# K and V caches loaded one head at a time, or two heads interleaved over the partitions: a decode block with sliding-window attention and a gated MLP

## The chip, the cores and the metric

The kernel runs on one core of one Trainium2 chip. The metric is the device time of one execution in microseconds (us). Each engine of the core has its own queue of instructions: PE multiplies matrices (PEld is its loading of the stationary operand), DVE is the vector engine, ACT the scalar engine, POOL the general engine, SP the sync engine, which here issues nearly all DMA transfers. One transfer is spread over 16 DMA engines. SBUF is the on-chip memory with 128 partitions, PSUM the memory that PE writes into.

## The reference

One token (a row x of 576 values) is normalised, goes through an attention block and through a gated MLP, and both results are added to x:

```
xn  = layernorm(x)                                   # 576
q   = xn @ wq                                        # 32 heads of 128
k,v = the last 4096 rows of each of 16 cached heads  # 128 columns, two q heads share one k, v head
p   = softmax(q . k / sqrt(128));  o = p @ v         # per head
A   = o (4096) @ wo                                  # 576
z   = gelu(xn @ w_in)                                # 4608, halves z1, z2
B   = (z1 * (w_sp * layernorm(z2) + b_sp)) @ w_out   # 2304 -> 576
out = x + A + B
```

All tensors are bfloat16. A cached head is a region of 65536 rows of 256 bytes, 16 MiB. Its last 4096 rows, 1 MiB, are read. K and V together are 33.5 MB of the 51 MB that the kernel reads; the rest is wq (4.7 MB), w_in (5.3 MB), wo (4.7 MB) and w_out (2.7 MB). A transfer's "row" below is the contiguous piece that one partition receives.

## The kernel before, in words

The order of the work is written out by hand. All large loads are issued by SP, in one queue and in a fixed order (lines 105 to 118): K of the first pair of heads, all of wq, then for each pair b = 1 to 8 the next K, the V of the pair before, and a piece of w_in (b = 1 to 3) or of wo (b = 4 to 6); after the last K come the last piece of wo, the last V, and w_out. Loads land in a pool of 18 units of one size (UNITS, line 34), taken in turn: a load waits until the unit's old content has been read. Besides, at most eight transfers are in flight at a time, which is how the kernel's tile library gives out its DMA semaphores.

`load_kv` (line 79) loads one head: partition p gets the 32 consecutive cache rows 32p to 32p+31, 8192 bytes. `load_rows` (line 92) loads two rows per partition of wq (8192 bytes) or of w_in (9216 bytes), or eight of w_out (9216 bytes), the last piece being smaller: one row of wq (4096 bytes) and of w_in (4608), two of w_out (2304).

Each pair of heads goes through these steps, in eight chunks n of eight 128x128 blocks:

- `T(n)` (line 199): eight transposes of K on PE into PSUM, then a copy to SBUF by DVE (five chunks of eight) or ACT (three). Three PSUM buffers serve all chunks.
- `S(n)` (line 210): eight matmuls with a transposed K block as the stationary operand and the two q columns of that head as the moving one. They fill the pair's score tile s, 128 partitions x (2 heads, 32 blocks, 2 queries).
- `sm_max`, `sm_tr`, `sm_exp`, `sm_rec` (lines 219 to 253): the maximum over the blocks (mx, DVE), over the partitions (a transpose on PE and a reduction), its broadcast by a small matmul (bc), then the difference d (DVE), the exponential p (ACT), the sums ss (DVE), and their total over the partitions by a matmul on PE (su), whose reciprocal is rm.
- `PV(b, i)` (line 255): 32 matmuls for head i of the pair, with a V block as the stationary operand and two columns of p as the moving one, accumulated in the tile o. `O(b)` scales it.

The main loop (lines 361 to 391) is a pipeline on PE: the transposes of pair b, with the scores of pair b two chunks behind, the total su of pair b-1 after the second chunk, then P V of pair b-1, whose second half hides the maximum of pair b, then in stages 1 to 3 `z_part(b)` (line 289: 18 matmuls for each row of w_in that has landed, four rows, four rows and one row), then the rest of pair b's softmax. Every second stage permutes the attention output (`O_perm`, tiles op and oP), and stages 4, 5, 6 and 8 multiply it with a piece of wo (`WO`). At the end 72 small matmuls (line 393) add the MLP's output from w_out's 18 rows, and the result is copied and stored. Before the loop, PE makes the eight chunks of the first pair and computes q row by row of wq (lines 336 to 341), 16 matmuls for each row.

Of the kernel before, what the change touches and what calls it, by code (L numbers as in the profile page):

```python
# [8 lines left out]
FP32 = mybir.dt.float32  # L9
BF16 = mybir.dt.bfloat16  # L10
ALU = mybir.AluOpType
ACT = mybir.ActivationFunctionType
AXX = mybir.AxisListType.X

P = 128
D = 576
HQ = 32
HKV = 16
DH = 128
SK = 65536  # L20
W = 4096
FH = 2304
NT = W // P
NB = HKV // 2
NCH = 8
NS = 9
# [4 lines left out]
OW = D // NCG  # L31
NWO = 4
FR = FH // P
UNITS = 18
KTB = 12


@with_exitstack
def kernel(
# [14 lines left out]
    nc = tc.nc  # L54
    ctx.enter_context(tc.manual_schedule())

    const = ctx.enter_context(tc.tile_pool(name="const", bufs=1))
    work = ctx.enter_context(tc.tile_pool(name="work", bufs=2))
    units = ctx.enter_context(tc.tile_pool(name="units", bufs=UNITS))
    ktp = ctx.enter_context(tc.tile_pool(name="ktp", bufs=KTB))  # L60
    PS = bass.MemoryType.PSUM
    ps_t = ctx.enter_context(tc.tile_pool(name="ps_t", bufs=3, space=PS))
    ps_s = ctx.enter_context(tc.tile_pool(name="ps_s", bufs=2, space=PS))
# [9 lines left out]
    kn, vn, wq_t, win_t, wo_t, wout_t = {}, {}, {}, {}, {}, {}  # L73
    wq_v = A_wq.rearrange("k (s c) -> (k s) c", s=2).rearrange("(p r) c -> p r c", r=NS)
    win_v = B_w_in.rearrange("k (s c) -> (k s) c", s=2).rearrange("(p r) c -> p r c", r=NS)
    wo_v = A_wo.rearrange("(j p r) n -> j p (r n)", p=P, r=8)
    wout_v = B_w_out.rearrange("(p r) n -> p r n", r=FR)

    def load_kv(store, cache, name, h):
        t = units.tile([P, NT, DH], BF16, name=f"{name}{h}", tag="u")  # L80
        nc.sync.dma_start(t[:], cache[0, h, SK - W:SK, :].rearrange("(p t) d -> p t d", p=P))
        store[h] = t

    def load_k(b):
        for i in range(2):
            load_kv(kn, A_k_cache, "k", 2 * b + i)

    def load_v(b):
        for i in range(2):
            load_kv(vn, A_v_cache, "v", 2 * b + i)  # L90

    def load_rows(store, view, name, width, rows, step):
        for a in range(rows.start, rows.stop, step):
            n = min(step, rows.stop - a)
            t = units.tile([P, step, width], BF16, name=f"{name}{a}", tag="u")
            nc.sync.dma_start(t[:, 0:n, :], view[:, a:a + n, :])
            for i in range(n):
                store[a + i] = t[:, i, :]

    def load_wo(j):  # L100
        t = units.tile([P, 8 * D], BF16, name=f"wo{j}", tag="u")
        nc.sync.dma_start(t[:], wo_v[j])
        wo_t[j] = t

    win_parts = {1: range(0, 4), 2: range(4, 8), 3: range(8, 9)}
    load_k(0)
    load_rows(wq_t, wq_v, "wq", 2048, range(0, NS), 2)
    for b in range(1, NB + 1):
        if b < NB:
            load_k(b)  # L110
        else:
            load_wo(NWO - 1)
        load_v(b - 1)
        if b in win_parts:
            load_rows(win_t, win_v, "win", FH, win_parts[b], 2)
        elif b < 7:
            load_wo(b - 4)
    load_rows(wout_t, wout_v, "wout", D, range(0, FR), 8)


    ident = const.tile([P, P], BF16, name="ident")
# [5 lines left out]
    ones_f = const.tile([P, P], FP32, name="ones_f")  # L127
    nc.vector.memset(ones_f[:], 1.0)
    ident_f = const.tile([P, P], FP32, name="ident_f")
# [2 lines left out]
    nc.vector.tensor_reduce(out=par[:], in_=ident_f[:].rearrange("p (m s) -> p s m", s=2), axis=AXX, op=ALU.add)  # L132
    hm = const.tile([P, 8], FP32, name="hm")
    nc.vector.tensor_reduce(out=hm[:], in_=ident_f[:].rearrange("p (n q) -> p n q", n=8), axis=AXX, op=ALU.add)
    selr = const.tile([P, 8, 8, 16], BF16, name="selr")
    out_ps = ps_c.tile([P, OW], FP32, name="out_ps")
    nc.vector.memset(out_ps[:], 0.0)
# [7 lines left out]
    for j in range(NS):  # L145
# [11 lines left out]
                                   op0=ALU.mult, op1=ALU.add, accum_out=stat[:, 1:2])  # L157
# [29 lines left out]
    def xe_of(r):  # L187
        return xe_r[:, 2 * r:2 * r + 2]
# [4 lines left out]
    kT, s_ps, p_sb, sm = {}, {}, {}, {}  # L193
    q_bf = const.tile([P, HQ], BF16, name="q_bf")
# [2 lines left out]
    ACT_COPIES = (1, 4, 6)  # L197

    def T(n):
        h, c = divmod(n, 4)  # L200
        kT[n] = ktp.tile([P, 8, P], BF16, name=f"kT{n}", tag="kT")
        tp = ps_t.tile([P, 8, P], BF16, name=f"tp{n}", tag="tp")
        for i in range(8):
            nc.tensor.transpose(tp[:, i, :], kn[h][:, 8 * c + i, :], ident[:])  # L204
        if n % 8 in ACT_COPIES:
            nc.scalar.copy(kT[n][:], tp[:])  # L206
        else:
            nc.vector.tensor_copy(kT[n][:], tp[:])  # L208

    def S(n):  # L210
        h, c = divmod(n, 4)
        b, i = divmod(h, 2)
        if n % NCH == 0:
            s_ps[b] = ps_s.tile([P, 2, NT, 2], FP32, name=f"s{b}", tag="s")
        for t in range(8):
            nc.tensor.matmul(s_ps[b][:, i, 8 * c + t, :], lhsT=kT[n][:, t, :], rhs=q_bf[:, 2 * h:2 * h + 2],  # L216
                             start=True, stop=True)

    def sm_max(b):
        mx = work.tile([P, 2, 2], FP32, name=f"mx{b}", tag="mx")  # L220
        nc.vector.tensor_reduce(out=mx[:], in_=s_ps[b][:].rearrange("p i t r -> p i r t"), axis=AXX, op=ALU.max)  # L221
        sm[b] = {"mx": mx}

    def sm_tr(b):
        tr = ps_m.tile([P, P], FP32, name=f"tr{b}", tag="m")
        nc.tensor.transpose(tr[0:4, :], sm[b]["mx"][:].rearrange("p i r -> p (i r)"), ident_f[:])  # L226
        m4 = work.tile([4, 1], FP32, name=f"m4{b}", tag="m4")
        nc.vector.tensor_reduce(out=m4[:], in_=tr[0:4, :], axis=AXX, op=ALU.max)  # L228
        dg = work.tile([4, 4], FP32, name=f"dg{b}", tag="dg")
        nc.vector.tensor_scalar_mul(dg[:], ident_f[0:4, 0:4], m4[:])  # L230
        sm[b]["dg"] = dg

    def sm_exp(b):
        bc = ps_m.tile([P, 4], FP32, name=f"bc{b}", tag="m")
        nc.tensor.matmul(bc[:], lhsT=ones_f[0:4, :], rhs=sm[b]["dg"][:], start=True, stop=True)  # L235
        mb = work.tile([P, 4], FP32, name=f"mb{b}", tag="mb")
        nc.vector.tensor_copy(mb[:], bc[:])
        d = work.tile([P, 2, NT, 2], FP32, name=f"d{b}", tag="d")
        m = mb[:].rearrange("p (i r) -> p i r", i=2).unsqueeze(2).to_broadcast([P, 2, NT, 2])
        nc.vector.tensor_tensor(out=d[:], in0=s_ps[b][:], in1=m, op=ALU.subtract)  # L240
        p = work.tile([P, 2, NT, 2], BF16, name=f"p{b}", tag="p")
        nc.scalar.activation(p[:], d[:], ACT.Exp, scale=SCALE)  # L242
        p_sb[b] = p
        ss = work.tile([P, 2, 2], FP32, name=f"ss{b}", tag="ss")
        nc.vector.tensor_reduce(out=ss[:], in_=p[:].rearrange("p i t r -> p i r t"), axis=AXX, op=ALU.add)  # L245
        sm[b]["ss"] = ss

    def sm_rec(b):
        su = ps_m.tile([P, 4], FP32, name=f"su{b}", tag="m")
        nc.tensor.matmul(su[:], lhsT=ones_f[:], rhs=sm[b]["ss"][:].rearrange("p i r -> p (i r)"), start=True, stop=True)  # L250
        rm = work.tile([P, 4], FP32, name=f"rm{b}", tag="rm")
        nc.vector.reciprocal(rm[:], su[:])
        sm[b]["rm"] = rm

    def PV(b, i):
        if i == 0:
            sm[b]["o"] = ps_o.tile([P, 4], FP32, name=f"o{b}", tag="o")
        for t in range(NT):
            nc.tensor.matmul(sm[b]["o"][:, 2 * i:2 * i + 2], lhsT=vn[2 * b + i][:, t, :], rhs=p_sb[b][:, i, t, :],  # L259
                             start=t == 0, stop=t == NT - 1)  # L260

    def O(b):
        with nc.allow_low_precision(reason="the attention's output is bfloat16 in the reference"):
# [23 lines left out]
    zacc = const.tile([P, FR, 2], FP32, name="zacc")  # L287

    def z_part(b):
        rows = win_parts[b]  # L290
        zp = ps_m.tile([P, FR, 2], FP32, name=f"zp{b}", tag="m")
        for r in rows:
            w_r = win_t[r].rearrange("p (m c) -> p c m", c=FR)
            for c in range(FR):
                nc.tensor.matmul(zp[:, c, :], lhsT=w_r[:, c, :], rhs=xe_of(r), start=(r == rows.start and c == 0),  # L295
                                 stop=r == rows.stop - 1, skip_group_check=True)
        if b == 1:
            nc.vector.tensor_copy(zacc[:], zp[:])
        else:
            nc.vector.tensor_tensor(out=zacc[:], in0=zp[:], in1=zacc[:], op=ALU.add)  # L300
# [60 lines left out]
    for b in range(1, NB + 1):  # L361
# [66 lines left out]
```

## Time and profile before

| what | value |
|---|---|
| median of 3 runs | 132.65 us (132.42 to 132.65) |
| the profiled execution | 132.56 us, its span 130.8 us |
| read from HBM | 50.96 MB, 390 GB/s over the span |
| PE busy, PEld busy | 103.5 us, 98.1 us |
| DVE, ACT busy | 51.8 us, 29.1 us |
| mean granted clock of PE | 0.73 of full speed |
| from issue to landing of a K or V transfer | 20.4 us |

The profile shows one execution. Its span begins with the first recorded instruction and ends with the last; 1.76 us of the execution's time lie outside it. The page cuts the span into 40 slices of 3.27 us. It gives each slice a digit for the busy share in tenths of every engine and of the DMA engines, the moved GB/s, and the granted clock of PE in tenths. The timeline lists instructions in the order of time (start, duration, engine, line, result <- operands, count); what stands in brackets is the engine's idle time before, and what ended it. A group's line gives the busy time, the mean of one in ns, and the idle time before. In the table of windows, the columns are the stretch, its length, busy time and count of PE, PEld, DVE, ACT and POOL, PE's granted clock, the DMA share and GB/s. A line of the waits reads: who waited, for whom, us in total, times, longest.

### The profile page before, as it was taken

What the parts mean: (1) busy time and instruction counts of PE and PEld (TensorE: products, weight loads), DVE (VectorE), ACT (ScalarE), POOL (GpSimd) and SP (SyncE); (2) the same over time, 40 slices, a digit from 0 to 9 for tenths busy, and PEclk for the clock granted to TensorE, in tenths of its full rate; (3) what the DMA queues carried; (4) which work ended last, traced back from release to release, by engine and by line L of the source; (5) the groups of instructions that cost most, each with busy time, mean ns of one, the idle gap of its engine ahead of it and who ended that gap; (6) DMA issues with size and microseconds to landing.
All of it is one profiled execution on the core that took longest, in us unless ns stands there. A gap on an engine that the chain in (4) does not pass through costs nothing.

```text
span 130.8 us, 4611 instructions
## 1 busy us (share of the span) xinstructions
PE 103.5 (79%) x2133; PEld 98.1 (75%) x2133; DVE 51.8 (40%) x157; ACT 29.1 (22%) x38; POOL 0.7 (1%) x6
## 2 busy tenths in 40 slices
PE   3587238699799998989977897899599869975760
PEld 3487227499698998989976896799499759964750
DVE  4495000345402543054537544654426434542100
ACT  3135000045000360005404140236025103500000
POOL 2000000000000000000000000000000000000000
PEclk9999955559955589657975568569959955995555
DMA  3999999999999999999999999999999999999820
GB/s 93 436 421 423 428 407 427 411 425 432 411 413 421 421 417 418 411 423 413 418 421 415 424 409 423 415 430 411 426 418 418 419 416 415 419 418 421 364 118 0
DMA packets 7088, 51.24 MB, mean 392 GB/s; under 512 B 797, under 2 KB 798, under 8 KB 1182
## 3 DMA queue, kind: packets, MB, share of 16 engines
q1 hardware_dynamic: 7064, 50.96, 94.2%
q8 instruction: 16, 0.26, 0.8%
q14 instruction: 2, 0.02, 0.0%
q10 hardware_dynamic: 6, 0.00, 0.0%
HBM read 50.96 MB, written 0.00 MB: 390 GB/s over the span
## 4 chain that ended last, share of the span: by engine, by line
DMA 63%; PE 31%; DVE 2%; issue 1%; SPq 0%
DMA k<-in_A_k_cache_dram 19%; DMA v<-in_A_v_cache_dram 17%; DMA wout<-in_B_w_out_dram 16%; PE tp L204 12%; DMA wq<-in_A_wq_dram 12%; PE zp L295 7%; PE s L216 4%; PE o L259 3%; PE bc L235 1%; PE out_ps L278 1%; PE su L250 1%; DVE m L228 1%; PE q_ps L339 0%; PE tr L226 0%; PE op L269 0%
## 5 line engine op out<-in xcount | busy, mean ns | idle before, releaser
L204 PE MATMUL tp<-ident,k 128*128 128x128 bf16 x512 | 50.1, 265 | 1.4 <-DMA k<-in_A_k_cache_dram 0.8
L204 PEld LDWEIGHTS <-k 128*128 128x128 bf16 x512 | 41.7, 123 | 2.9 <-issue 2.0
L208 DVE COPY kT<-tp 128x1024 bf16<-128x1024 bf16 x40 | 27.5, 690 | 21.1 <-PE tp L204 20.9
L206 ACT COPY kT<-tp 128x1024 bf16<-128x1024 bf16 x24 | 24.2, 1011 | 32.1 <-PE tp L204 32.1
L216 PE MATMUL s<-q_bf,kT 128*128 128x2 bf16 x512 | 20.6, 165 | 1.3 <-DVE kT L208 1.1
L216 PEld LDWEIGHTS <-kT 128*128 128x128 bf16 x512 | 19.1, 101 | 1.6 <-DVE kT L208 1.4
L259 PE MATMUL o<-p,v 128*128 128x2 bf16 x512 | 15.3, 163 | 1.0 <-DMA v<-in_A_v_cache_dram 0.5
L259 PEld LDWEIGHTS <-v 128*128 128x128 bf16 x512 | 14.3, 97 | 1.2 <-DMA v<-in_A_v_cache_dram 0.6
L242 ACT ACTIVATE p<-d 128x128 bf16<-128x128 f32 x8 | 2.5, 309 | 50.9 <-DVE d L240 50.9
L295 PEld LDWEIGHTS <-win 128*128 128x128 bf16 x162 | 10.5, 163 | 1.5 <-issue 1.5
L295 PE MATMUL zp<-xe,win 128*128 128x2 bf16 x162 | 10.4, 200 | 1.1 <-DVE m L228 1.1
L339 PE MATMUL q_ps<-xe,wq 128*128 128x2 bf16 x144 | 4.5, 165 | 5.4 <-DMA wq<-in_A_wq_dram 5.4
L339 PEld LDWEIGHTS <-wq 128*128 128x128 bf16 x144 | 4.1, 101 | 5.8 <-DMA wq<-in_A_wq_dram 5.8
L235 PEld LDWEIGHTS bc<-dg,ones_f 4*128 4x128 f32 x16 | 3.3, 253 | 5.4 <-DVE dg L230 4.2
L235 PE MATMUL bc<-dg,ones_f 4*128 4x4 f32 x16 | 4.0, 318 | 4.0 <-DVE dg L230 3.1
L278 PE MATMUL out_ps<-wo,oP 128*1 128x144 bf16 x128 | 4.6, 308 | 2.3 <-DVE oP L274 1.6
L250 PEld LDWEIGHTS su<-ss,ones_f 128*128 128x128 f32 x16 | 4.3, 332 | 1.4 <-DVE ss L245 1.4
L250 PE MATMUL su<-ss,ones_f 128*128 128x4 f32 x16 | 4.3, 341 | 1.3 <-DVE ss L245 1.3
L278 PEld LDWEIGHTS <-oP 128*1 128x1 bf16 x128 | 3.1, 110 | 2.7 <-DVE oP L274 1.8
L221 DVE TENSOR_REDUCE mx<-s 128x4 f32<-128x128 f32 x8 | 2.3, 292 | 6.8 <-PE s L216 6.8
L341 DVE CAST q_bf<-q_ps 128x32 bf16<-128x32 f32 x1 | 0.3, 303 | 9.1 <-PE q_ps L339 9.1
L264 DVE TENSOR_TENSOR oTn<-o,rm 128x4 bf16<-128x4 f32 x8 | 1.3, 162 | 6.4 <-PE o L259 6.4
(78 smaller groups left out, 42.0 us busy)
## 6 DMA issues: line engine op xcount, KB each, us to landing
k<-in_A_k_cache_dram SPq DMA_DIRECT2D x16, 1024.0 KB, 20.4
v<-in_A_v_cache_dram SPq DMA_DIRECT2D x16, 1024.0 KB, 20.5
win<-in_B_w_in_dram SPq DMA_DIRECT2D x4, 1152.0 KB, 18.9
wo<-in_A_wo_dram SPq DMA_DIRECT2D x4, 1152.0 KB, 19.8
wq<-in_A_wq_dram SPq DMA_DIRECT2D x4, 1024.0 KB, 14.3
wout<-in_B_w_out_dram SPq DMA_DIRECT2D x2, 1152.0 KB, 20.4
win<-in_B_w_in_dram SPq DMA_DIRECT2D x1, 576.0 KB, 19.4
wq<-in_A_wq_dram SPq DMA_DIRECT2D x1, 512.0 KB, 15.1
```

The costliest lines, as they stand in the source:

```text
L204: nc.tensor.transpose(tp[:, i, :], kn[h][:, 8 * c + i, :], ident[:])
L206: nc.scalar.copy(kT[n][:], tp[:])
L208: nc.vector.tensor_copy(kT[n][:], tp[:])
L216: nc.tensor.matmul(s_ps[b][:, i, 8 * c + t, :], lhsT=kT[n][:, t, :], rhs=q_bf[:, 2 * h:2 * h + 2], start=True, stop=True)
L221: nc.vector.tensor_reduce(out=mx[:], in_=s_ps[b][:].rearrange("p i t r -> p i r t"), axis=AXX, op=ALU.max)
L235: nc.tensor.matmul(bc[:], lhsT=ones_f[0:4, :], rhs=sm[b]["dg"][:], start=True, stop=True)
L242: nc.scalar.activation(p[:], d[:], ACT.Exp, scale=SCALE)
L250: nc.tensor.matmul(su[:], lhsT=ones_f[:], rhs=sm[b]["ss"][:].rearrange("p i r -> p (i r)"), start=True, stop=True)
L259: nc.tensor.matmul(sm[b]["o"][:, 2 * i:2 * i + 2], lhsT=vn[2 * b + i][:, t, :], rhs=p_sb[b][:, i, t, :], start=t == 0, stop=t == NT - 1)
L278: nc.tensor.matmul(out_ps[32 * g:32 * g + 1, :], lhsT=lhsT, rhs=rhs[:, OW * g:OW * (g + 1)], start=start, stop=last, tile_position=(0, 32 ...
L295: nc.tensor.matmul(zp[:, c, :], lhsT=w_r[:, c, :], rhs=xe_of(r), start=(r == rows.start and c == 0), stop=r == rows.stop - 1, skip_group_c ...
L339: nc.tensor.matmul(q_ps[:, c, :], lhsT=wq_t[r][:, P * c:P * (c + 1)], rhs=xe_of(r), start=(r == 0 and c == 0), stop=r == NS - 1, skip_grou ...
```

## The change

Two heads are loaded by one transfer: even partitions hold the first head of the pair, odd ones the second, and each partition gets 64 consecutive cache rows, 16384 bytes. A transposed block of K therefore has columns of both heads. The scores are computed for the four queries of the pair against every column; before them, one matmul per pair fills the score tile with -1e30 where a query meets the other head's column and with 0 elsewhere, and the scores are accumulated on top. After the exponential, the masked places are 0, so P V runs over 64 blocks with four columns each and needs no separation. The score, difference and p tiles are twice as wide. A pair has as many transposes, score matmuls and P V matmuls as before.

The units are now 10, each large enough for 16384 bytes. wq comes in pieces of 4, 4 and 1 rows, w_in in three pieces of 3 rows, w_out in pieces of 8, 6, 3 and 1 rows. `z_part` follows w_in's pieces.

```diff
-NT = W // P
+NT = 2 * W // P
-UNITS = 18
+UNITS = 10
+NEG = -1e30
...
-    def load_kv(store, cache, name, h):
-        t = units.tile([P, NT, DH], BF16, name=f"{name}{h}", tag="u")
-        nc.sync.dma_start(t[:], cache[0, h, SK - W:SK, :].rearrange("(p t) d -> p t d", p=P))
-        store[h] = t
+    def load_kv(store, cache, name, b):
+        t = units.tile([P, NT, DH], BF16, name=f"{name}{b}", tag="u")
+        nc.sync.dma_start(t[:].rearrange("p t d -> p (t d)"),
+                          cache[0, 2 * b:2 * b + 2, SK - W:SK, :].rearrange("a (i t) d -> i a (t d)", t=NT))
+        store[b] = t
...
-    def load_rows(store, view, name, width, rows, step):
-        for a in range(rows.start, rows.stop, step):
-            n = min(step, rows.stop - a)
-            t = units.tile([P, step, width], BF16, name=f"{name}{a}", tag="u")
-            nc.sync.dma_start(t[:, 0:n, :], view[:, a:a + n, :])
+    def load_rows(store, view, name, width, cuts):
+        for a, e in zip(cuts, cuts[1:]):
+            t = units.tile([P, e - a, width], BF16, name=f"{name}{a}", tag="u")
+            nc.sync.dma_start(t[:], view[:, a:e, :])
...
-    win_parts = {1: range(0, 4), 2: range(4, 8), 3: range(8, 9)}
+    win_parts = {1: (0, 3), 2: (3, 6), 3: (6, 9)}
-    load_rows(wq_t, wq_v, "wq", 2048, range(0, NS), 2)
+    load_rows(wq_t, wq_v, "wq", 2048, (0, 4, 8, 9))
-            load_rows(win_t, win_v, "win", FH, win_parts[b], 2)
+            load_rows(win_t, win_v, "win", FH, win_parts[b])
-    load_rows(wout_t, wout_v, "wout", D, range(0, FR), 8)
+    load_rows(wout_t, wout_v, "wout", D, (0, 8, 14, 17, 18))
...
+    own = const.tile([2, P], BF16, name="own")
+    nc.vector.tensor_copy(own[:].rearrange("a (i c) -> a i c", c=2), ident[0:2, 0:2].unsqueeze(1).to_broadcast([2, P // 2, 2]))
+    neg = const.tile([2, 2], FP32, name="neg")
+    nc.vector.tensor_scalar(out=neg[:], in0=ident[0:2, 0:2], scalar1=1.0, scalar2=-NEG, op0=ALU.subtract, op1=ALU.mult)
+    other = const.tile([2, NT * 4], BF16, name="other")
+    nc.vector.tensor_copy(other[:].rearrange("a (t h r) -> a t h r", h=2, r=2),
+                          neg[:].unsqueeze(1).unsqueeze(3).to_broadcast([2, NT, 2, 2]))
...
     def S(n):
-        h, c = divmod(n, 4)
-        b, i = divmod(h, 2)
-        if n % NCH == 0:
-            s_ps[b] = ps_s.tile([P, 2, NT, 2], FP32, name=f"s{b}", tag="s")
+        b, c = divmod(n, NCH)
+        if c == 0:
+            s_ps[b] = ps_s.tile([P, NT, 4], FP32, name=f"s{b}", tag="s")
+            nc.tensor.matmul(s_ps[b][:].rearrange("p t c -> p (t c)"), lhsT=own[:], rhs=other[:],
+                             start=True, stop=False, skip_group_check=True)
         for t in range(8):
-            nc.tensor.matmul(s_ps[b][:, i, 8 * c + t, :], lhsT=kT[n][:, t, :], rhs=q_bf[:, 2 * h:2 * h + 2],
-                             start=True, stop=True)
+            nc.tensor.matmul(s_ps[b][:, 8 * c + t, :], lhsT=kT[n][:, t, :], rhs=q_bf[:, 4 * b:4 * b + 4],
+                             start=False, stop=True, skip_group_check=True)
...
     def PV(b, i):
-        for t in range(NT):
-            nc.tensor.matmul(sm[b]["o"][:, 2 * i:2 * i + 2], lhsT=vn[2 * b + i][:, t, :], rhs=p_sb[b][:, i, t, :],
-                             start=t == 0, stop=t == NT - 1)
+        for t in range(NT // 2 * i, NT // 2 * (i + 1)):
+            nc.tensor.matmul(sm[b]["o"][:], lhsT=vn[b][:, t, :], rhs=p_sb[b][:, t, :], start=t == 0, stop=t == NT - 1)
```

The softmax helpers change in the shape of their tiles alone (128 x 64 x 4 in place of 128 x 2 x 32 x 2).

More of the change, by code (lines that the diff above doesn't have):

```diff
@@ L77 @@
     wout_v = B_w_out.rearrange("(p r) n -> p r n", r=FR)
-    def load_kv(store, cache, name, h):
-        t = units.tile([P, NT, DH], BF16, name=f"{name}{h}", tag="u")
-        nc.sync.dma_start(t[:], cache[0, h, SK - W:SK, :].rearrange("(p t) d -> p t d", p=P))
-        store[h] = t
+    def load_kv(store, cache, name, b):
[3 more added lines that the diff above has]
+        store[b] = t
     def load_k(b):
-        for i in range(2):
-            load_kv(kn, A_k_cache, "k", 2 * b + i)
+        load_kv(kn, A_k_cache, "k", b)
     def load_v(b):
-        for i in range(2):
-            load_kv(vn, A_v_cache, "v", 2 * b + i)
-    def load_rows(store, view, name, width, rows, step):
-        for a in range(rows.start, rows.stop, step):
-            n = min(step, rows.stop - a)
-            t = units.tile([P, step, width], BF16, name=f"{name}{a}", tag="u")
-            nc.sync.dma_start(t[:, 0:n, :], view[:, a:a + n, :])
-            for i in range(n):
-                store[a + i] = t[:, i, :]
+        load_kv(vn, A_v_cache, "v", b)
+    def load_rows(store, view, name, width, cuts):
+        for a, e in zip(cuts, cuts[1:]):
+            t = units.tile([P, e - a, width], BF16, name=f"{name}{a}", tag="u")
+            nc.sync.dma_start(t[:], view[:, a:e, :])
+            for i in range(a, e):
+                store[i] = t[:, i - a, :]
     def load_wo(j):
@@ L203, in T @@
         for i in range(8):
-            nc.tensor.transpose(tp[:, i, :], kn[h][:, 8 * c + i, :], ident[:])
+            nc.tensor.transpose(tp[:, i, :], kn[b][:, 8 * c + i, :], ident[:])
         if n % 8 in ACT_COPIES:
@@ L210, in S @@
     def S(n):
-        h, c = divmod(n, 4)
-        b, i = divmod(h, 2)
-        if n % NCH == 0:
-            s_ps[b] = ps_s.tile([P, 2, NT, 2], FP32, name=f"s{b}", tag="s")
+        b, c = divmod(n, NCH)
+        if c == 0:
+            s_ps[b] = ps_s.tile([P, NT, 4], FP32, name=f"s{b}", tag="s")
+            nc.tensor.matmul(s_ps[b][:].rearrange("p t c -> p (t c)"), lhsT=own[:], rhs=other[:],
+                             start=True, stop=False, skip_group_check=True)
         for t in range(8):
-            nc.tensor.matmul(s_ps[b][:, i, 8 * c + t, :], lhsT=kT[n][:, t, :], rhs=q_bf[:, 2 * h:2 * h + 2],
-                             start=True, stop=True)
+            nc.tensor.matmul(s_ps[b][:, 8 * c + t, :], lhsT=kT[n][:, t, :], rhs=q_bf[:, 4 * b:4 * b + 4],
+                             start=False, stop=True, skip_group_check=True)
     def sm_max(b):
-        mx = work.tile([P, 2, 2], FP32, name=f"mx{b}", tag="mx")
-        nc.vector.tensor_reduce(out=mx[:], in_=s_ps[b][:].rearrange("p i t r -> p i r t"), axis=AXX, op=ALU.max)
+        mx = work.tile([P, 4], FP32, name=f"mx{b}", tag="mx")
+        nc.vector.tensor_reduce(out=mx[:], in_=s_ps[b][:].rearrange("p t c -> p c t"), axis=AXX, op=ALU.max)
         sm[b] = {"mx": mx}
@@ L225, in sm_tr @@
         tr = ps_m.tile([P, P], FP32, name=f"tr{b}", tag="m")
-        nc.tensor.transpose(tr[0:4, :], sm[b]["mx"][:].rearrange("p i r -> p (i r)"), ident_f[:])
+        nc.tensor.transpose(tr[0:4, :], sm[b]["mx"][:], ident_f[:])
         m4 = work.tile([4, 1], FP32, name=f"m4{b}", tag="m4")
@@ L237, in sm_exp @@
         nc.vector.tensor_copy(mb[:], bc[:])
[L238 to L241, printed above, removed]
+        d = work.tile([P, NT, 4], FP32, name=f"d{b}", tag="d")
+        nc.vector.tensor_tensor(out=d[:], in0=s_ps[b][:], in1=mb[:].unsqueeze(1).to_broadcast([P, NT, 4]), op=ALU.subtract)
+        p = work.tile([P, NT, 4], BF16, name=f"p{b}", tag="p")
         nc.scalar.activation(p[:], d[:], ACT.Exp, scale=SCALE)
         p_sb[b] = p
-        ss = work.tile([P, 2, 2], FP32, name=f"ss{b}", tag="ss")
-        nc.vector.tensor_reduce(out=ss[:], in_=p[:].rearrange("p i t r -> p i r t"), axis=AXX, op=ALU.add)
+        ss = work.tile([P, 4], FP32, name=f"ss{b}", tag="ss")
+        nc.vector.tensor_reduce(out=ss[:], in_=p[:].rearrange("p t c -> p c t"), axis=AXX, op=ALU.add)
         sm[b]["ss"] = ss
@@ L249, in sm_rec @@
         su = ps_m.tile([P, 4], FP32, name=f"su{b}", tag="m")
-        nc.tensor.matmul(su[:], lhsT=ones_f[:], rhs=sm[b]["ss"][:].rearrange("p i r -> p (i r)"), start=True, stop=True)
+        nc.tensor.matmul(su[:], lhsT=ones_f[:], rhs=sm[b]["ss"][:], start=True, stop=True)
         rm = work.tile([P, 4], FP32, name=f"rm{b}", tag="rm")
@@ L289, in z_part @@
     def z_part(b):
-        rows = win_parts[b]
+        rows = range(win_parts[b][0], win_parts[b][-1])
         zp = ps_m.tile([P, FR, 2], FP32, name=f"zp{b}", tag="m")
```

## The prediction

> **What bounds the kernel now.** I read the slices of the page first, then the queue of the sync engine, then PE's waits and the tail, because two things run nearly level here: the DMA stream and PE.
>
> ```profile
> PE 103.5 (79%) x2133; PEld 98.1 (75%) x2133; DVE 51.8 (40%) x157; ACT 29.1 (22%) x38; POOL 0.7 (1%) x6
> ...
> DMA  3999999999999999999999999999999999999820
> GB/s 93 436 421 423 428 407 427 411 425 432 411 413 421 421 417 418 411 423 413 418 421 415 424 409 423 415 430 411 426 418 418 419 416 415 419 418 421 364 118 0
> ...
> q1 hardware_dynamic: 7064, 50.96, 94.2%
> q8 instruction: 16, 0.26, 0.8%
> ```
>
> The queues are full from slice 2 to slice 37 at about 418 GB/s. What moves the stream is its rate, not the moment at which a load is issued. The next view is the sync engine's timeline, cut into short windows. With eight transfers in flight, each issue waits for the landing of the transfer eight places ahead, so the distance of two issues is the time that one transfer takes in the stream.
>
> ```profile
> 61.94 0.33 SPq L81 DMA_DIRECT2D k<-in_A_k_cache_dram  x1
> 63.35 0.33 SPq L81 DMA_DIRECT2D v<-in_A_v_cache_dram  x1
> ...
> 95.34 0.33 SPq L102 DMA_DIRECT2D wo<-in_A_wo_dram  x1
> 97.83 0.33 SPq L81 DMA_DIRECT2D v<-in_A_v_cache_dram  x1
> 100.33 0.33 SPq L81 DMA_DIRECT2D v<-in_A_v_cache_dram  x1
> 103.10 0.33 SPq L96 DMA_DIRECT2D wout<-in_B_w_out_dram  x1
> ```
>
> Eight transfers back stand w_in's last piece (4608-byte rows, 63.35 - 61.94 = 1.41 us), two halves of V (8192-byte rows, 100.33 - 97.83 = 2.50) and w_o (9216-byte rows, 103.10 - 100.33 = 2.77). Now PE. These are its waits from 60 us on, the groups of the softmax, and the timeline of the tail:
>
> ```profile
> PE out_ps L278 <- DMA wout<-in_B_w_out_dram: 1.3, 1, 1.3
> PE o L259 <- DMA v<-in_A_v_cache_dram: 0.5, 1, 0.5
> ```
> ```profile
> L242 ACT ACTIVATE p<-d 128x128 bf16<-128x128 f32 x8 | 2.5, 309 | 50.9 <-DVE d L240 50.9
> L221 DVE TENSOR_REDUCE mx<-s 128x4 f32<-128x128 f32 x8 | 2.3, 292 | 6.8 <-PE s L216 6.8
> ```
> ```profile
> 118.83 0.59 PE L250 MATMUL su<-ss,ones_f 128*128 128x4 f32 x2 [1.30 <-DVE ss L245]
> 119.28 0.99 PE L259 MATMUL o<-p,v 128*128 128x2 bf16 x32
> 120.77 1.01 PE L259 MATMUL o<-p,v 128*128 128x2 bf16 x32 [0.50 <-DMA v<-in_A_v_cache_dram]
> 122.96 1.13 PE L278 MATMUL out_ps<-wo,oP 128*1 128x144 bf16 x32 [0.57 <-DVE oP L274]
> 123.88 1.18 PE L278 MATMUL out_ps<-wout,hv 128*1 128x144 bf16 x32
> 126.35 1.37 PE L278 MATMUL out_ps<-wout,hv 128*1 128x144 bf16 x40 [1.29 <-DMA wout<-in_B_w_out_dram]
> ```
>
> In the last 70 us PE waits for data only twice, 1.8 us together. The chain of waits gives DMA 63%, but PE follows 1.8 us behind. A faster stream alone can therefore win no more than about that. PE's own pace is set by its granted clock:
>
> ```profile
> 104.60:111.40 6.80, 5.53 (x84) 5.21 (x84) 2.66 (x8) 1.32 (x2) 0.00 (x0) 0.50 1.01 418
> 111.40:118.30 6.90, 5.50 (x158) 5.21 (x155) 3.45 (x9) 2.17 (x3) 0.00 (x0) 0.99 1.01 419
> ```
>
> Column 8 is the clock. In the chain of waits eight transposes take 0.88 us at 0.5 and 0.47 us at 1.0. The clock records change only at multiples of 3.41 us from one another, up after a stretch filled with transposes, down after one of small matmuls.
>
> **The change part by part.** *Longer rows.* The trace's packet records have one packet per row: medians 160 ns for 4096 bytes, 312 for 8192, 349 for 9216, and 9 ns for each completion packet. From 4096 to 9216 that is 0.0369 ns a byte and 9 ns a packet. An engine takes 8 rows and one completion per transfer, so a transfer costs about 0.08 us beside its bytes. The issue distances put this between 0.02 (1.41 and 2.77) and 0.10 (2.50 and 2.77). K and V go from 32 transfers to 16 (16 x 0.08 = 1.3 us less), w_q from 5 to 3 (0.16), w_in from 5 to 3 (0.16), w_out from 3 to 4 (0.08 more). The sum is 1.5 us less, between 0.4 and 1.9. V's last half, for which PE now waits until 120.77, lands near 119.2. The last piece of w_out (issued at 108.06, landed 19.0 us later at 127.0) lands near 125.5.
>
> *No early starvation.* A unit is now 16 KB, and 10 replace 18. Transfer n needs the unit of n-10. The nearest case is late: the last w_out piece needs K6, whose transposes end near 101 us; its bytes move after 125. No reuse wait should empty the queue. The first pair of K lands near 8.2 us instead of 5.7; its eight chunks (5.8 us in the trace) still end before w_q is complete at 20.9. That wait is the cover. DVE builds the mask's two operands ahead of the normalisation: three small operations, 0.2 to 0.3 us each by the rows of that stretch, so xe is ready near 8.1 us instead of 7.3; its first reader, w_q's first matmul, runs at 11.6 now and later after. Free as well.
>
> *PE at the start.* w_q's second piece holds four rows. After it lands (about 19.3), 64 + 16 matmuls at 0.03 us end near 21.75, against 21.45 now: 0.3 us later.
>
> *The mask.* Eight matmuls of 256 columns. By the transposes (128 columns in 0.11 or 0.06 us) each is 0.22 or 0.12 us; seven lie on PE's path, 1.2 us. Scores and P V keep their counts; they get 4 columns instead of 2, and both stand at 0.02 us each whatever the clock, so nothing is added.
>
> *The softmax at double width.* 64 against 128 elements on DVE: 218 (om) and 292 ns, so 256 cost 0.15 more; ACT's 309 ns against 1011 for 1024 elements gives 0.10. mx lies beside P V (0.8 us) except at the first pair, 0.13 there. d, p and ss lie beside two chunks of transposes, 1.7 us; if that cover is gone, su starts up to 0.1 us later in each stage. At the last pair nothing covers them: 0.15 + 0.10 + 0.15 = 0.4.
>
> *w_in in 3 + 3 + 3 rows instead of 4 + 4 + 1.* A row costs PE 1.15 us (4.59 for four). Stages 1 and 2 get shorter, stage 3 gets 2.3 longer, no net change.
>
> *PE's sum.* Serial: 0.3 + 0.13 + 1.2 + up to 0.5 + 0.4 = 2.1 to 2.5. The clock rises at fixed moments, so a later start loses time at the slow pace: a delay of 0.41 of every 0.88 us is returned at the next rise. About half of each delay survives a stage, and the delays of some 0.2 us a stage settle at 0.4. Missing a rise by a little costs one interval at the slow pace, 3.41 x 0.47 = 1.6; catching an earlier one returns as much. I take 0.4 + 0.4 (tail) = 0.8 us, between -0.8 and 4.1.
>
> *The tail.* The last P V starts at 119.28 + 0.8 = 120.1, after V's landing (119.2). 64 matmuls at the present pace (2 x 0.85) end at 121.8; the head's permutation takes 1.34 (121.62 to 122.96), w_o 0.92, so w_out starts near 124.1; its 72 matmuls at 0.034 (40 in 1.37) end at 126.55. The last piece has landed by then; with one row of four matmuls it would allow 125.7. Today the end is 127.72. So 1.2 us less: 132.56 - 1.2 = 131.4 against the profiled execution, whose span is 130.8 with 1.76 around it; the median of the runs is 0.09 higher, hence 131.5.
>
> **Against the change.** In every load of the trace a transfer walks one contiguous region; rows from two heads, 16 MiB apart, in one transfer are not shown. The bounds are the slowest stretch of the steady slices (407 GB/s) and the rate by the packet fit (2097152 bytes in 4.89 us, 429 GB/s). I take the fit, because 9216-byte rows already lie on it. [...]
>
> **The rivals.** First, the other side: the two-head transfer runs below the present rate. For it: nothing in the trace excludes it. Against: the slices hold 407 to 436 GB/s whatever is loaded. It decides where the last V lands after 121.25 (120.1 + 1.2), that is where a pair takes over 5.02 us instead of 4.89. At 407 GB/s a pair takes 5.15, the last V lands at 119.2 + 16 x 0.26 = 123.4, 3.3 us after 120.1, and the time is 134.8; for worse rows the trace gives no end. Second: PE takes over fully. It misses one rise of the clock (1.6): 133.1; with the serial sum of 2.3 in place of 0.8 as well, 134.6. For it: only 1.8 us of waiting is left. Against: stages 1 and 2 get shorter. Third: a packet costs next to nothing, 0.4 us of stream in all: V lands at 120.3, the last row at 126.6, the time is 131.7. Fourth: PE's delay is fully absorbed, and P V starts at 119.3, just behind V's landing: 130.7.
>
> **How the numbers follow.** The measurement can tell about 0.2%, 0.27 us. Forecast, with its own range 130.3 to 132.3: 0.50. Third and fourth rivals: 0.13 together, both faster. PE takes over: 0.19, of which 0.09 lies within 0.2% of before (a delay 1.1 us above my 0.8). The slower stream: 0.18. Faster 0.63, same 0.09, slower 0.28. The range is 130.0 to 134.2: below it lies little, above it most of the slower stream.
>
> **What would show it.** The page after should list 8 + 8 issues of 2048 KB for K and V, distances of 4.9 us between their landings, some 430 GB/s in the K and V slices, and near 4,300 packets on the queue of the loads. PE should wait less than 0.5 us for V and for w_out in the tail, and its su of the last pair should stand between 118.5 and 120.5. Issue distances above 5.02 us would prove me wrong by the first rival, a su after 121 by the second.

## The result, and the profile after

The changed kernel is slower: 137.59 us, the median of 6 executions (136.43 to 142.55), against 132.49 us (132.37 to 132.65) for the kernel before, a ratio of 1.036 with a 95% interval of 1.032 to 1.041. Executions more than 1.5% above the fastest of their kernel are left out of such ratios and their intervals, while the medians and ranges in this text hold every execution.

The profiled execution took 137.67 us, with a span of 135.9. First the page's engine line, the slices (3.40 us each) and the queue of the loads:

```profile
PE 108.1 (80%) x2141; PEld 100.4 (74%) x2141; DVE 55.5 (41%) x160; ACT 30.0 (22%) x38; POOL 0.7 (1%) x6
...
PEclk9999965555865555558975557757977975797555
DMA  2999999999999999999999999999999999994000
GB/s 78 424 424 444 410 444 415 434 414 430 444 410 415 439 417 434 423 410 451 410 414 430 439 415 409 447 413 439 417 427 429 422 407 435 409 395 161 5 0 0
...
q1 hardware_dynamic: 4328, 50.96, 89.0%
```

The stream did what was forecast. There are 4328 packets instead of 7064, no slice is empty before the end, and the loads are over in slice 37. By the trace's completion records the last V has landed at 119.6 us (120.7 before) and the last piece of w_out at 125.8 (127.0 before). Two-head transfers that follow each other land 4.89 us apart; a packet of 16384 bytes has a median of 612 ns.

But the execution ends 10 us after the stream. Here is the end of PE's timeline:

```profile
126.08 0.59 PE L259 MATMUL su<-ss,ones_f 128*128 128x4 f32 x2 [1.67 <-DVE ss L254]
126.53 1.85 PE L268 MATMUL o<-p,v 128*128 128x4 bf16 x64
129.56 1.13 PE L286 MATMUL out_ps<-wo,oP 128*1 128x144 bf16 x32 [0.57 <-DVE oP L282]
130.47 2.38 PE L286 MATMUL out_ps<-wout,hv 128*1 128x144 bf16 x72
```

The total su of the last pair starts at 126.1 instead of 118.8. V has been there since 119.6, and the last piece of w_out, which PE reaches at 130.5, since 125.8; nothing in this stretch waits for a load. The chain of waits says the same: it was 63% DMA and is now

```profile
PE 69%; DMA 13%; DVE 10%; issue 3%; ACT 1%; SPq 1%; ACTq 0%
```

Where did PE's 7.3 us come from? The transposes of stage 1 start 0.8 us later (26.84 for 26.07). From there to the last su, 92.8 us have become 99.2. Added up by the distance from one matmul's start to the next, the 6.5 us are: the mask 2.0; the transposes 2.1, of which 1.4 because 269 of the 448 run at the slow clock, not 241; the parts that wait for DVE (bc, op, the gate of the MLP) 1.6; the rest 0.8. Most of the other 0.7 of the transposes belongs to the mask: at the slow clock PE takes 0.25 us from the last transpose ahead of it to the mask, where one transpose follows another after 0.11. So a two-row mask costs 0.43 us at the slow clock and 0.32 at the fast one, about 2.3 us in stages 1 to 3 and 5 to 7; in stage 4 it lies beside a wait for a copy of K. The waits of PE from 60 us on show the third part, and a line of the rest:

```profile
PE bc L245 <- DVE dg L240: 2.5, 4, 0.6
PE out_ps L286 <- DVE oP L282: 2.0, 2, 1.4
PE su L259 <- DVE ss L254: 1.7, 1, 1.7
PE o L268 <- issue: 1.1, 1, 1.1
...
PE op L277 <- DVE mz L172: 0.9, 1, 0.9
```

The waits for oP (1.6 before) and for the gate (mz, 0.5 before) have grown, because they stand behind ss on DVE, and ss (420 ns for 286 before) waits for the longer d (424 for 291) and p (416 for 309). No load is in this list. The line with "issue" is a wait in P V for which the profile names no releaser. Such waits differ between executions: after 20 us they come to 1.4 us here, 1.2 before, and 0 to 2.9 in the profiles of the runs below. All 28 of them end 2.36 to 2.64 us after the start of a 16 KB packet on the instruction queue. That PE waits for its instructions there is the author's reading of this and not shown. The mean granted clock of the whole execution is 0.692 (0.730 before).

### The profile page after: what moved, and what is told of

Same layout as the page of the kernel before. It is cut to its first block, busy times and chain, and to the rows that moved or that the text cites. A ratio compares the mean times of both kernels' runs of the same rounds, so it can differ in the third digit from the quotient of the medians.

```text
span 135.9 us, 4599 instructions
## 1 busy us (share of the span) xinstructions
PE 108.1 (80%) x2141; PEld 100.4 (74%) x2141; DVE 55.5 (41%) x160; ACT 30.0 (22%) x38; POOL 0.7 (1%) x6
## 3 DMA queue, kind: packets, MB, share of 16 engines
q1 hardware_dynamic: 4328, 50.96, 89.0%
## 4 chain that ended last, share of the span: by engine, by line
PE 69%; DMA 13%; DVE 10%; issue 3%; ACT 1%; SPq 1%; ACTq 0%
PE tp L213 27%; DMA wq<-in_A_wq_dram 13%; PE o L268 10%; PE s L226 10%; PE zp L303 8%; PE out_ps L286 5%; PE bc L245 3%; PE su L259 2%; PE q_ps L347 2%; DVE m L238 2%; PE s L223 1%; DVE d L249 1%; ACT p L251 1%; DVE ss L254 1%; DVE oTn L272 1%
## 5 line engine op out<-in xcount | busy, mean ns | idle before, releaser
L213 PE MATMUL tp<-ident,k 128*128 128x128 bf16 x512 | 51.8, 270 | 3.9 <-DMA k<-in_A_k_cache_dram 3.9
L213 PEld LDWEIGHTS <-k 128*128 128x128 bf16 x512 | 42.8, 126 | 5.4 <-DMA k<-in_A_k_cache_dram 3.9
L226 PE MATMUL s<-q_bf,kT 128*128 128x4 bf16 x512 | 20.9, 166 | 1.0 <-DVE kT L217 1.0
L268 PE MATMUL o<-p,v 128*128 128x4 bf16 x512 | 15.3, 165 | 1.1 <-issue 1.1
L251 ACT ACTIVATE p<-d 128x256 bf16<-128x256 f32 x8 | 3.3, 416 | 52.2 <-DVE d L249 52.2
L303 PE MATMUL zp<-xe,win 128*128 128x2 bf16 x162 | 10.4, 200 | 1.1 <-DVE m L238 1.1
L245 PEld LDWEIGHTS bc<-dg,ones_f 4*128 4x128 f32 x16 | 3.8, 293 | 5.4 <-DVE dg L240 4.2
L245 PE MATMUL bc<-dg,ones_f 4*128 4x4 f32 x16 | 4.5, 349 | 4.0 <-DVE dg L240 3.1
L347 PE MATMUL q_ps<-xe,wq 128*128 128x2 bf16 x144 | 4.0, 164 | 4.2 <-DMA wq<-in_A_wq_dram 4.2
L231 DVE TENSOR_REDUCE mx<-s 128x4 f32<-128x256 f32 x8 | 3.4, 424 | 7.0 <-PE s L226 7.0
L254 DVE TENSOR_REDUCE ss<-p 128x4 f32<-128x256 bf16 x8 | 3.4, 420 | 4.1 <-ACT p L251 4.1
```

The source lines that it names most:

```text
L213: nc.tensor.transpose(tp[:, i, :], kn[b][:, 8 * c + i, :], ident[:])
L226: nc.tensor.matmul(s_ps[b][:, 8 * c + t, :], lhsT=kT[n][:, t, :], rhs=q_bf[:, 4 * b:4 * b + 4], start=False, stop=True, skip_group_check=True)
L254: nc.vector.tensor_reduce(out=ss[:], in_=p[:].rearrange("p t c -> p c t"), axis=AXX, op=ALU.add)
L268: nc.tensor.matmul(sm[b]["o"][:], lhsT=vn[b][:, t, :], rhs=p_sb[b][:, t, :], start=t == 0, stop=t == NT - 1)
```

## The experiments

In the short diffs, a line with "after" or "before" says which kernel they are made from. The kernel before ran beside each of them: 132.2 to 133.0 us, with medians of 132.4 to 132.6.

### The mask in PE's idle time

```diff
 after
+    def mask(b):   # the matmul own x other into the score tile of pair b
     def S(n):
-            nc.tensor.matmul(s_ps[b][:].rearrange("p t c -> p (t c)"), lhsT=own[:], rhs=other[:], ...)
...
             sm_tr(b)
+            if b + 1 < NB: mask(b + 1)
```

> The changed kernel, with each pair's mask matmul moved from between the transposes into the wait of PE behind the transpose of the maxima, where it stands idle for 0.4 to 0.6 us. Theory serial: the mask costs its own time, 2.0 us in stages 1 to 7, and the clock does not care: 135.6 us, granted clock 0.69 as now. Theory gate: the mask among the transposes also lets stretches of 3.41 us fall short of what raises the clock; with it gone the clock rises at the first full stretch again: 133 to 134.5 us, mean clock 0.71 to 0.73. Theory landings (PE waits because pairs land late): 137.5, unchanged.

Measured: 133.85 us (133.65 to 134.41, 4 executions), clock 0.716 to 0.726. The changed kernel's executions had 0.679 to 0.707. Its ratio to the kernel before is 1.010 (1.008 to 1.013). The place of eight small matmuls is worth 3.7 us by the medians. Landings are not the cause. The expectation put the mask's own time at 2.0 us; with the 2.3 from above, the serial theory covers most of the 3.2 us by which the last su comes earlier in the profile (122.9 for 126.1). That profile shows no faster transposes: 264 of the 448 run at the slow clock, 269 in the changed kernel. It is the slowest of the four executions; the others have the higher clock, 0.726, and are 0.5 to 0.8 us faster.

### The same mask with 128 rows

```diff
 after
-    own = const.tile([2, P], BF16, name="own")
-    other = const.tile([2, NT * 4], BF16, name="other")
+    own, other: 128 partitions, zeros from row 2 on
```

> The changed kernel, the mask matmul at its old place but with 128 rows of zeros and masks instead of 2: the same time on PE, more of the array in use. Theory serial: 137.6, unchanged. Theory gate, if what counts is how many rows of the array work: the clock rises as early as without the mask and the time falls to 134.5 to 136; if what counts is only time or columns, it stays at 137.6.

Measured: 135.42 us (133.18 to 136.29, 4 executions), ratio 1.011 (1.003 to 1.019), clock 0.733 to 0.766 in the four. The clock is higher than in any execution of the changed kernel. But the padded mask is also shorter in effect, which the durations hide. Here is one chunk of eight transposes of stage 2, the mask behind it and the next chunk, at the slow clock in both; the changed kernel first, then the one with 128 rows:

```profile
44.59 1.01 PE L213 MATMUL tp<-ident,k 128*128 128x128 bf16 x8
45.53 0.39 PE L223 MATMUL s<-other,own 2*128 2x256 bf16 x1
...
46.09 1.01 PE L213 MATMUL tp<-ident,k 128*128 128x128 bf16 x8
```
```profile
43.81 1.01 PE L215 MATMUL tp<-ident,k 128*128 128x128 bf16 x8
44.62 0.42 PE L225 MATMUL s<-other,own 128*128 128x256 bf16 x1
...
45.09 1.01 PE L215 MATMUL tp<-ident,k 128*128 128x128 bf16 x8
```

From chunk to chunk it is 1.50 us with two rows, 1.28 with 128 and 1.07 without a mask. So the padding saves 0.22 us a stage at this clock, about 1.2 in all, before any change of the clock. The two tables of windows show the start of stage 2 in each (the last three columns are the clock, the DMA share and GB/s), in the same order:

```profile
42.45:45.41 2.96, 2.96 (x27) 2.82 (x26) 1.78 (x5) 1.43 (x2) 0.00 (x0) 0.50 1.01 428
45.41:48.83 3.42, 3.42 (x50) 3.08 (x49) 1.38 (x2) 0.63 (x1) 0.00 (x0) 0.50 1.03 439
48.83:52.24 3.41, 3.41 (x75) 3.41 (x74) 1.38 (x2) 1.40 (x2) 0.00 (x0) 0.50 0.98 408
```
```profile
41.68:46.81 5.13, 5.13 (x59) 5.00 (x59) 3.15 (x7) 1.43 (x2) 0.00 (x0) 0.50 1.04 439
46.81:53.63 6.82, 5.76 (x160) 5.54 (x158) 2.46 (x7) 2.02 (x2) 0.00 (x0) 1.00 0.99 417
```

With two rows, the whole stage of transposes (42.45 to 51.2) is done at half the clock. With 128 rows the clock rises 5.1 us after the stage's start. In the two lines of the changed kernel from 45.41 to 52.24 PE is 100% busy and the clock stays at half; in the first line of the other it is 100% busy too, and the clock rises behind it. So the busy share did not tell here when the clock rose. In the whole profile 211 of the 448 transposes run at the slow clock, 269 in the changed kernel; that is 3.0 us. With the 1.2 us above, and 1.5 us more of waits without a releaser against it, this sums to 2.7 us; su comes 2.75 us earlier (123.33 for 126.08).

What stood ahead of a rise of the clock can be counted in the profiles of the two kernels and all twelve runs. The clock's changes lie on a grid of 3.41 us in every profile. Counting the transposes that start in each stretch of the grid that runs at the slow clock, from stage 1 to the last su, gives:

| transposes started in a stretch of 3.41 us at half the clock | such stretches | followed by the full clock |
|---|---|---|
| 25 to 27 | 52 | 52 |
| 22 to 24 | 44 | 32 |
| 21 or fewer | 131 | 8 |

No stretch with a two-row mask among its transposes held more than 24: 14 such stretches, 6 of them followed by the full clock. At half the clock the mask takes the room of four transposes with two rows (0.43 us against 0.11 each) and of two with 128 (0.21). That it acts on the clock through this room is the author's inference from the counts; whether the rows count by themselves is not separated from it.

### No mask matmul at all

```diff
 after
-            nc.tensor.matmul(s_ps[b]..., lhsT=own[:], rhs=other[:], start=True, stop=False, ...)
...
-        nc.tensor.matmul(bc[:], lhsT=ones_f[0:4, :], rhs=sm[b]["dg"][:], start=True, stop=True)
+        nc.tensor.matmul(bc[:], lhsT=lhs6[:], rhs=sm[b]["dg"][:], start=True, stop=True)
```

Rows 4 and 5 of lhs6 hold the two heads' partition patterns, rows 4 and 5 of dg hold 1e30 where a query meets the other head. The maxima are then taken over both heads' keys, which the softmax allows.

> The changed kernel without any mask matmul: the mask comes in with the broadcast of the maxima (two more rows in that matmul, K of 6 instead of 4), so that the difference d already holds -1e30 at the other head's places. PE has the same matmuls per pair as the kernel before. Theory serial: 135.6. Theory gate: 132.5 to 134, as with the mask in the gap. If it is still above 135, neither the mask nor its place is the cause, and the later start and the wider softmax are.

Measured: 135.01 us, but from 131.95 to 136.01 in 10 executions, clock 0.713 to 0.746; ratio 1.003 (0.999 to 1.007). It is faster than the changed kernel. Against the run with the mask in the gap the two measures disagree: its median is higher, its ratio lower (1.003 for 1.010). The median is nearer the serial theory's number, the ratio, which stands for some 132.9 us, lies in the other's range, so this run does not decide between them. In its profile su stands at 122.5: without the mask, PE is still 3.6 us behind the kernel before, so there is more than the mask. Stages 1 and 2 together took 0.8 us less than before, stage 3 took 3.3 more.

### The rows of w_in as before

```diff
 the kernel without a mask matmul
-    win_parts = {1: (0, 3), 2: (3, 6), 3: (6, 9)}
+    win_parts = {1: (0, 3, 4), 2: (4, 7, 8), 3: (8, 9)}
```

> The run without any mask matmul, with w_in's rows given back to the stages as before: 4 in the first, 4 in the second, 1 in the third (as pieces of 3, 1, 3, 1 and 1 rows). Theory that moving rows between stages nets nothing: 135.0 us, the median of that run. Theory that it does not: stages 1 and 2 gave back only 0.8 us of the 2.3 that they should have, and stage 3 lost 3.3, so the time falls by 1 to 2.5 us, to 132.5 to 134.

Measured: 133.40 us (131.70 to 136.08, 10 executions), ratio 1.002 (1.000 to 1.005). The median falls by 1.6 us, as the second theory says, but the ratio is that of the run above (1.003), so a gain is not shown.

### The mask alone, in the kernel before

```diff
 before
+            nc.tensor.matmul(<256 columns of the score bank>, lhsT=own[:], rhs=other[:], start=True, stop=True)
```

Here `other` holds zeros.

> The kernel before with one part of the change alone: a matmul of the mask's shape (2 rows, 256 columns) ahead of each pair's scores; the scores then overwrite what it wrote. Theory serial: 2.0 us more on PE, of which 1.8 were waiting for the stream: 132.5 to 133. Theory gate: 3.5 to 4 us more on PE, as its removal gave in the changed kernel, so 133.5 to 135 and a lower mean clock than the 0.70 to 0.75 of the kernel before.

Measured: 135.49 us (132.94 to 141.65, 6 executions), clock 0.614 to 0.711, ratio 1.011 (1.007 to 1.015). One part of the change alone takes the kernel before out of its narrow range and slows its median by 3.0 us. The loads are those of the kernel before, one head each. In the profile, which is of the fastest execution, su comes 2.5 us later than before (121.3), no more than the mask's own price. The slower executions go with a lower clock: 132.94 us at 0.711, 134.31 and 134.59 at 0.701, 136.40 at 0.681, 137.04 at 0.677 and 141.65 at 0.614. Together with the run with the mask in the gap this shows that the mask's matmul, at this place, costs 3 to 4 us by the medians, of which 2.3 to 2.5 are its own. That the rest is the clock's is inferred from this order, not measured by itself.

### The parts that touch the stream alone

```diff
 before
-    load_rows(wout_t, wout_v, "wout", D, range(0, FR), 8)
+    load_rows(wout_t, wout_v, "wout", D, range(0, 14), 8)
+    load_rows(wout_t, wout_v, "wout", D, range(14, 17), 8)
+    load_rows(wout_t, wout_v, "wout", D, range(17, FR), 8)
```

> The kernel before with w_out's end in finer pieces alone (8, 6, 3 and 1 rows). There the stream sets the end: one row instead of ten is left to multiply after the last landings, so 0.4 us less, 132.1. If PE sets the end there too: 132.5, unchanged.

Measured: 132.07 us (131.99 to 132.21, 5 executions), ratio 0.996 (0.995 to 0.998). The finer end is worth what the tail's lines said, 0.47 us. Its clock went from 0.699 to 0.747 and the time stayed. Note its su in the profiled execution, 1.8 us later than in the profile of before, with the same matmuls up to there:

```profile
120.67 0.59 PE L252 MATMUL su<-ss,ones_f 128*128 128x4 f32 x2 [1.30 <-DVE ss L247]
125.05 2.38 PE L280 MATMUL out_ps<-wout,hv 128*1 128x144 bf16 x72
```

So the 1.8 us of waiting in the profile of before, at a clock of 0.730, were those of one execution; in this one, at 0.699, PE waits neither for V nor for w_out and has hardly any room.

### Less for PE to do, in both kernels

First the order: the permutation of the attention output (O_perm) ahead of the rest of the softmax, so that oP no longer stands behind ss on DVE. In the two-head kernel w_q's pieces were also made finer.

```diff
 the kernel without a mask matmul, w_in 4, 4, 1 (x7) | before, with w_out's finer end (x8)
+        if b % 2 == 0: O_perm(b // 2 - 1)
         if b < NB: sm_exp(b)
...
-        if b % 2 == 0: O_perm(b // 2 - 1)
 x7 only
-    load_rows(wq_t, wq_v, "wq", 2048, (0, 4, 8, 9))
+    load_rows(wq_t, wq_v, "wq", 2048, (0, 4, 6, 8, 9))
```

> As the run before it (no mask matmul, w_in 4, 4, 1), with w_q in pieces of 4, 2, 2 and 1 rows, and the permutation of the attention output ahead of the rest of the softmax, so that the second wait of PE on DVE in stages 4 and 6 (1.0 and 1.4 us) goes. If PE sets the end of the changed kernel, each of these shows in the time: su of the last pair at 119 to 121 us, and the end set by the stream, whose last landing stays at 125.8: 130.9 to 131.8 us, faster than both kernels. If something else of the two-head transfers costs time, it stays above 132.5.

> The kernel before with the finer end of w_out and the same earlier permutation, nothing else. There the stream sets the end, so PE's gain of 1 to 2 us is worth nothing: 132.1, as with the finer end alone. Below 131.7 would mean that PE was on the path before as well.

Measured: the two-head kernel 132.71 us (131.70 to 133.91, 12 executions, ratio 1.001, 0.999 to 1.003), still not below the kernel before; the one-head kernel 132.06 (131.91 to 132.20, 5), just as with the finer end alone. The control came out as expected. The first did not: its last su stands at 121.6, so PE is still its end, only nearer.

Then a real relief. The 162 matmuls of w_in take every 18th column as the stationary operand. With every third column instead, and w_out's rows in runs of three to match, the result is the same.

```diff
-            w_r = win_t[r].rearrange("p (m c) -> p c m", c=FR)
+            w_r = win_t[r].rearrange("p (k m u) -> p k u m", k=6, u=3)
...
-    wout_v = B_w_out.rearrange("(p r) n -> p r n", r=FR)
+    wout_v = B_w_out.rearrange("(k p u) n -> p k (u n)", k=6, u=3)
 w_out in pieces of 9, 6, 2, 1 rows (two heads) or 6, 6, 3, 2, 1 (one head)
```

The relief went into the two-head kernel with the earlier permutation, into the kernel before with the same, and into the changed kernel as it stands:

> The two-head version without a mask matmul, with w_in's 162 matmuls made cheaper: their stationary operand takes every third column of w_in instead of every eighteenth, and w_out's rows are loaded in runs of three (3456 bytes) to match. A matmul of w_in stands at 0.069 us now, one of w_q, whose columns lie side by side, at 0.030: PE saves between 0 (if only neighbouring columns are fast) and 5.8 us. The stream loses 24 packets of 9 ns an engine, 0.2 us. If PE is what held the two-head version back, the stream now sets the end: last landing near 126.0, 131.1 us, in every run within 0.3. If it stays at 132.7 with spread, either the price of w_in's matmuls is unchanged or the stream is not the floor that I take it for.

> The kernel before with the same cheaper matmuls of w_in, the earlier permutation and a fine end of w_out. Its stream keeps one head and 8192-byte rows to a transfer, so if the stream is its floor, PE's gain is worth nothing: 132.1 to 132.3. The distance to the two-head version, 1.0 to 1.2 us, is then what the longer rows are worth.

> The changed kernel as it is, mask among the transposes, 3 rows of w_in a stage, with the cheaper matmuls of w_in alone. If PE is on its path from end to end, the whole gain shows: 137.6 less 4 to 6 is 131.6 to 133.6 us. If it waits for the landings of the pairs, nothing or little shows: 136 or more.

Measured: 131.22 us (131.18 to 131.29, 5 executions), 132.17 (132.09 to 132.32, 10), and 133.59 (131.65 to 135.65, 10), with ratios of 0.990, 0.997 and 0.997. All three came out where they must if PE ends the changed kernel. The group of w_in in the two-head kernel:

```profile
L311 PE MATMUL zp<-xe,win 128*128 128x2 bf16 x162 | 4.7, 165 | 1.1 <-DVE m L246 1.1
```

It was 10.4 us busy. And its tail, in which PE waits for V again:

```profile
118.79 0.59 PE L267 MATMUL su<-ss,ones_f 128*128 128x4 f32 x2 [1.68 <-DVE ss L262]
119.85 1.86 PE L276 MATMUL o<-p,v 128*128 128x4 bf16 x64 [0.47 <-DMA v<-in_A_v_cache_dram]
122.89 1.13 PE L294 MATMUL out_ps<-wo,oP 128*1 128x144 bf16 x32 [0.57 <-DVE oP L290]
123.80 2.56 PE L294 MATMUL out_ps<-wout,hv 128*1 128x144 bf16 x72
```

The executions agree within 0.1 us again, at clocks from 0.723 to 0.760. So did those of the kernel before with the finer end alone, within 0.22 us at 0.699 to 0.747. The same relief gave the one-head kernel nothing (132.17 us, 132.06 without it), because its stream was its end already. In its tail PE waits for both halves of V, longer than before:

```profile
118.27 1.01 PE L264 MATMUL o<-p,v 128*128 128x2 bf16 x32 [1.02 <-DMA v<-in_A_v_cache_dram]
120.79 1.01 PE L264 MATMUL o<-p,v 128*128 128x2 bf16 x32 [1.51 <-DMA v<-in_A_v_cache_dram]
```

The difference of the two, 0.95 us, is what the two-head loads, with the mask folded into the broadcast and the finer pieces, are worth once PE has room; the last landing is 1.2 us earlier (126.0 for 127.2).

### Fewer transfers

```diff
 the two-head kernel with the relief
-    w_q in pieces of 4, 2, 2, 1 rows, w_in in 3, 1 / 3, 1 / 1
+    w_q in pieces of 4, 4, 1 rows, w_in in 3 / 3 / 3
```

> The two-head version with the cheaper matmuls of w_in, now with the changed kernel's own pieces of w_q (4, 4, 1 rows) and w_in (3, 3, 3), three transfers fewer. By 0.08 us a transfer the stream ends 0.24 us earlier: 131.0 us, if PE, with 3 rows of w_in moved to stage 3 and w_q finished 0.3 us later, still has the room. If PE has not, the spread of several tenths comes back and the median lies above 131.3.

Measured: 130.96 us (130.81 to 131.49, 5 executions), ratio 0.990 (0.988 to 0.992), beside a kernel before that ran at 132.37 in that comparison. The ratio is that of the run above, 0.990 (0.988 to 0.991), so the 0.24 us are not shown. Either version is 1.0% faster than the kernel before and 4.6 to 4.8% faster than the changed one.

## Why the prediction was wrong

The forecast was 131.5 with a range from 130.0 to 134.2 and a chance of 0.28 for slower; the time is 137.6. Of the prediction's own signs, those of the stream came true, and so did the one against it, an su after 121.

- *The stream.* Right. A gain of 1.5 us was forecast, and the landings came 1.2 earlier; the first bytes moved 0.4 later (2.19 for 1.76 us), and the rate gave the rest, 1.6 us for 19 transfers fewer, near the 0.08 a transfer that the packets said. The bounds were worked out wrongly: the two pairs of issue distances that the prediction names give 0.05 and 0.34 us by a straight line, not 0.02 and 0.10. The first rival, a loss through the two heads' distance, did not happen: pairs land 4.89 us apart, as forecast.
- *The tail.* Right as far as it is about the stream: a finer end is worth 0.47 us where the stream ends the kernel. In the changed kernel it is worth nothing, since every piece has landed before PE comes to it.
- *PE's sum.* This step failed. It took 0.8 us (-0.8 to 4.1); the last su came 7.3 us later. The start of stage 1 came 0.8 us later, where its terms gave 0.4. The mask's term was too small, what stands behind ss on DVE was left out, and the clock's part was worked out from moments that do not stand still; the next points take these one by one. The waits without a releaser were in no term either: 0.2 us more in this pair of profiles, up to 2.9 in one of the runs.
- *"About half of each delay survives a stage, and the delays of some 0.2 us a stage settle at 0.4."* Wrong. It let the raised clock's moments stand still and only the work move. By the table above, whether the clock rose at all went with the work: after all 52 stretches with 25 or more transposes, after 8 of 131 with 21 or fewer. The mask was priced by its columns (1.2 us); it cost 2.3 in its own time and, taken out of the transposes, gave back 3.7 by the medians, with a higher clock. In the profile of after, the transposes of stages 1 and 2 run almost wholly at half speed (0.50 from 26.84 to 35.18 us and from 42.45 to 52.24).
- *"w_in in 3 + 3 + 3 rows, no net change."* Neither confirmed nor refuted: with the old rows the median is 1.6 us lower, the ratio the same. In one pair of profiles the stages that got shorter did not give back their share.
- *The softmax at double width "lies beside".* For ss and su it does. But DVE's queue holds, behind ss, the permutation's two operations and the MLP's gate, and PE waits for these in stages 4 and 6. The prediction did not ask what is queued behind ss. It is 0.8 us of the waits shown above.
- *"PE follows 1.8 us behind."* That was one execution. In the profiles of two runs with the same PE work up to that point, or a little less, su came at 120.5 to 120.7, so there was next to no room. A median that does not move from execution to execution hides that PE's part of it does.
- *The second rival*, PE takes over fully, was the right one; its price (133.1 to 134.6) was too small, as it had one missed rise of the clock and the serial sum with the mask at 1.2 us.

What stays open: how much each of the terms has in the 5.1 us, since the variants that PE ends spread over 1 to 9 us, and why the run without any mask spreads over 4 us, with a median above that of the run with the mask in PE's idle time. Its clock does not order its times (136.01 us at 0.713, but 135.45 at 0.738 and 133.20 at 0.723); the waits without a releaser vary too (0 to 2.9 us), but only one execution of each run was profiled.

## What to carry to other kernels

Where two resources run level, relieve the second one before speeding up the first: here the faster stream was worth 1.0 us only after PE had been given some 5 us of room. See how the time behaves over several executions together with the granted clock: here, times that agreed within 0.1 to 0.3 us while the clock varied by 0.03 to 0.05 were those of variants that the stream ended, and the variants that spread over 2 us or more were all ended by PE. A small spread alone is no proof: the run with the mask in the gap, which PE ends too, moved by 0.8 us. The mask's matmul of two rows, put among transposes, cost more here than its columns say (0.43 us at half the clock, 0.21 with 128 rows), and no stretch of 3.41 us at that clock with it held more than 24 transposes, where others held up to 27; so put such a matmul where PE stands idle, or fold its work into a matmul that is there anyway.

## What the runs showed of the hardware that was not expected

- The clock did not follow PE's busy share: at 100% busy it rose after some stretches (the mask with 128 rows, 41.68 to 46.81 us) and not after others (the changed kernel, 45.41 to 48.83). All 52 stretches of 3.41 us with 25 or more transposes were followed by the full clock, 8 of 131 with 21 or fewer (these eight held 16 to 21 transposes and 20 to 35 other matmuls).
- The mask's matmul with 2 rows between matmuls with 128 took 0.43 us of PE's time at half the clock, the same one padded with zeros to 128 rows 0.21. The mean granted clock went with it from 0.679-0.707 to 0.733-0.766.
- PE stands in 28 waits that name no releaser, in 13 of the 14 profiles, 0.16 to 1.6 us each. All of them end 2.36 to 2.64 us after the start of a packet on the instruction queue.
- The clock changed at multiples of 3.41 us from one another, but at other moments in each execution: in the first four two-head kernels profiled, which all start their transposes at 8.4 to 8.6 us, the first rise came at 11.3, 13.0, 12.7 and 12.1 us. The clock rises eight times in the profile of before and seven times in that of after, and one program that PE ends, the one without a mask matmul and with the rows of w_in as before, took 131.7 to 136.1 us (10 executions, 3.3%). How much of this spread is the clock's is not shown.
- With a stationary operand whose columns lie 36 bytes apart, a matmul of w_in stood at 0.062 us from start to start (median); at 6 bytes it was 0.027, close to the 0.026 of w_q, whose columns lie side by side.
- In the profile of before, the instruction queue moved 16 packets of 16 KB, each of 1.0 to 1.1 us. The 16 completions of a transfer lie within 0.5 us there at first, 1.9 us from the first of these packets on (15.1 us) and 3.4 us from the ninth on (76.8 us); the last full w_out piece ends between 122.98 and 126.31. That the packets are the cause is not shown.
